# Grouped-query attention on a cache: K loaded in 32 KiB rows, two units in interleaved partitions, with another load order

## The chip, the cores and the metric

The kernel runs on one core of a Trainium2 chip. The metric is the device time of one execution in microseconds (us); less is better. The core has five engines that run side by side, each through its own list of instructions in order: TensorE (PE, matrix products), VectorE (DVE), ScalarE (ACT), GpSimd (POOL) and SyncE (SP), which here issues every transfer between the chip's main memory (HBM) and the on-chip memory (SBUF, 128 partitions). The transfers are carried out by sixteen DMA engines that all work on one queue: each transfer is dealt out over them, and each works through its share of one transfer after the other. TensorE's results land in a small memory of their own, PSUM.

## The reference

Eight sequences (B), four new tokens each (Sq), 32 query heads that share 8 key/value heads, a cache of 2048 keys (Sk), head size 128, bf16:

```python
q = (x @ wq).reshape(B, Sq, Hq, Dh).transpose(0, 2, 1, 3)
k = jnp.repeat(k_cache, rep, axis=1)          # rep = 4
v = jnp.repeat(v_cache, rep, axis=1)
scores = jnp.einsum("bhqd,bhkd->bhqk", q, k) * (Dh ** -0.5)
p = softmax(scores, axis=-1)
o = jnp.einsum("bhqk,bhkd->bhqd", p, v)
out = o.transpose(0, 2, 1, 3).reshape(B, Sq, Hq * Dh) @ wo
```

k_cache and v_cache are 33.5 MB each, wq and wo 4.2 MB each: 75.5 MB are read in all.

## The kernel before

**Units.** The work is cut into 16 units (NU). A unit is one sequence b and four key/value heads (G = 4, one half hq of the eight), so 64 rows of queries (NQ: 4 heads, 4 repeats, 4 tokens) against 2048 keys per head. Its K is 2 MiB, and so is its V. In SBUF, partition (g, s) of a K or V load holds 64 consecutive keys of head g (C = 64 keys of 128 numbers, 16 KiB in one run).

**Stages of a unit.** (1) `turn_keys` (L141): VectorE turns K in blocks of 32 by 32, seen as 4-byte pairs, two tiles of 32 keys per partition. (2) `scores` (L211): per tile eight matmuls of 512 columns against the block-diagonal queries `q_bd`; the two halves of a tile go to PSUM partitions 0 to 63 and 64 to 127. (3) `maxima` (L232) on VectorE: the row maximum, two small copies that swap the halves, and one operation that makes the bias `less`. (4) `exponentials` (L251) on ScalarE, with the row sums. (5) `probs_to_keys` (L262): one turn of the probabilities on VectorE, then eight copies, half on ScalarE and half on GpSimd, into a block-diagonal `probs` buffer (two of them). (6) `values` (L297): 32 matmuls on TensorE in four quarters. (7) `divide` (ScalarE) by the row sums, whose reciprocals `inverses` (VectorE) makes from `sums` (GpSimd); `finish` turns the result back (one or two matmuls and a copy).

**Order.** The order of the instructions on each engine is the order in which the program writes them (the scheduler is switched to manual). The loop at L394 runs over n: it turns and scores unit n, spreads the probabilities of unit n - 1, takes the maxima and exponentials of n, and does the values of unit n - 2 (LAG = 2). Unit 0's two tiles are turned ahead of the loop, L148.

**Loads.** All go through SP's queue in program order, and an instruction of SP that waits holds up those behind it. K has three buffers of one unit (KB), V three (VB). The list `loads` (L115) alternates K and V, K of unit u ahead of V of unit u - 2, and `load_ready` issues each as soon as the program has passed the last use of its buffer; K0, wq, x and one load of K1 with K2 are issued ahead. x lands in one of the three buffers of turned keys. After the last V the output weights wo follow in pieces, in the memory that wq had (L433).

**End.** `project` (L382) multiplies by wo, piece by piece in the order of the loads, once the last unit is finished and turned to rows (`to_tokens`, `to_wo_rows`).

Of the kernel before, what the change touches and what calls it, by code (L numbers as in the profile page):

```python
# [14 lines left out]
def kernel(  # L15
# [23 lines left out]
    NT, CT = 2, C // 2  # L39
# [5 lines left out]
    KB, VB, PB, LAG = 3, 3, 2, 2  # L45
# [11 lines left out]
    vpool = ctx.enter_context(tc.tile_pool(name="vpool", bufs=VB))  # L57
# [11 lines left out]
    x_sb = ktpool.tile([128, CT, 2, S, 2], BF16, tag="kt", name="x_sb")  # L69
# [12 lines left out]
    ks = [None] * NU  # L82
    vs = [None] * NU

    k_sb = kpool.tile([128, KB, C, Dh], BF16, name="k_sb")

    def load_k(u, n=1):
        hq, b = units[u]
        nc.sync.dma_start(
            k_sb[:, u % KB : u % KB + n, :, :].rearrange("p b c d -> p b (c d)"),  # L90
            k_cache[b : b + n, G * hq : G * hq + G].rearrange(
                "b g (s c) d -> (g s) b (c d)", c=C
            ),
        )
        for i in range(n):
            ks[u + i] = k_sb[:, (u + i) % KB, :, :]

    def load_v(u):
        hq, b = units[u]
        vs[u] = vpool.tile([128, C, Dh], BF16, tag="v_sb", name="v_sb")  # L100
        of = v_cache[b, G * hq : G * hq + G].rearrange("g (s c) d -> (g s) c d", c=C)
        nc.sync.dma_start(vs[u][:, :, :], of)
# [8 lines left out]
    x_all = x_sb[:T, :, :, :, :].rearrange("q c h s e -> q (c h s e)")  # L111
    nc.vector.memset(x_all, 0.0)  # L112
    nc.sync.dma_start(x_all[::XR, :], x.flatten_outer_dims().rearrange("(a i) d -> a (i d)", i=XR))
    load_k(1, 2)
    loads = [("v", 0)]  # L115
    for u in range(3, NU + 2):
        if u < NU:
            loads.append(("k", u))
        loads.append(("v", u - 2))
    loads.reverse()  # L120

    def load_ready(nk, nv):
        while loads:
            kind, u = loads[-1]
            if u >= (nk + KB if kind == "k" else nv + VB):
                return
            (load_k if kind == "k" else load_v)(u)
            loads.pop()

    load_ready(0, 0)  # L130
# [10 lines left out]
    def turn_keys(u, t):  # L141
        kts[(u, t)] = ktpool.tile([128, CT, 2, S, 2], BF16, tag="kt", name="kt")
        nc.vector.transpose(  # L143
            kts[(u, t)][:, :, :, :, :].rearrange("k c h s e -> k (c h s e)").bitcast(FP32),
            ks[u][:, t * CT : (t + 1) * CT, :].rearrange("s c d -> s (c d)").bitcast(FP32),
        )

    for t in range(NT):  # L148
        turn_keys(0, t)
# [12 lines left out]
    nc.vector.tensor_copy(out=xT_sb[:, :, :], in_=xtp[:, :, :])  # L162

# [47 lines left out]
    def scores(u, t):  # L211
        hq, b = units[u]
        if t == 0:
            s_pss[u] = psum_s.tile([128, NT, CT // 2, S], FP32, tag="s", name="s_ps")
        for i in range(4):
            k, e = i // 2, i % 2
            for h in range(2):
                nc.tensor.matmul(  # L218
                    s_pss[u][h * NQ : (h + 1) * NQ, t, :, :],
                    lhsT=q_bd[:, hq, k, e, b, :, :].rearrange("k g q -> k (g q)"),  # L220
                    rhs=kts[(u, t)][:, h * CT // 2 : (h + 1) * CT // 2, k, :, e],
                    start=(i == 0),
                    stop=(i == 3),
                )
# [7 lines left out]
    def maxima(u):  # L232
# [5 lines left out]
            in_=s_pss[u][:, :, :, :].rearrange("q t c s -> q (t c s)"),  # L238
# [12 lines left out]
    def exponentials(u):  # L251
# [3 lines left out]
            out=s_sbs[u][:, :, :, :].rearrange("q a s j -> q a j s"),  # L255
            in_=s_pss[u][:, :, :, :].rearrange("q t (a j) s -> q (t a) j s", j=2),
# [5 lines left out]
    def probs_to_keys(u):  # L262
        p_t = small.tile([128, C // 4, 2, HQ, 2], BF16, tag="p_t", name="p_t")
        nc.vector.transpose(  # L264
            p_t[:, :, :, :, :].rearrange("s x g q j -> s (x g q j)").bitcast(FP32),
            s_sbs[u][:, :, :, :].rearrange("q a s j -> q (a s j)").bitcast(FP32),
        )
        by = [nc.scalar.copy, nc.gpsimd.tensor_copy] * G
        if u == NU - 1:
            by = [nc.vector.tensor_copy, nc.gpsimd.tensor_copy, nc.scalar.copy] * 3  # L270
        for h in range(2):
            for g in range(G):
# [3 lines left out]
                    in_=p_t[quad * S : (quad + 1) * S, :, g % 2, :, :].rearrange(  # L276
# [20 lines left out]
    def values(u, quarter):  # L297
        if quarter == 0:
            o_pss[u] = psum_o.tile([128, 2, Dh], FP32, tag="o", name="o_ps")
        t, h = quarter // 2, quarter % 2  # L300
        for a in range(CT // 4):
# [3 lines left out]
                lhsT=probs[u % PB][:, h, t * CT // 4 + a, :, :, :].rearrange(  # L305
# [87 lines left out]
    pieces = [(0, 0, 8), (1, 0, 8), (2, 0, 8), (3, 0, 5), (3, 5, 2), (3, 7, 1)]  # L393
    for n in range(NU + LAG):  # L394
        w = n - LAG
        if 0 < n <= NU:
            total = sums(n - 1)
        if 0 < n < NU:
            turn_keys(n, 0)
            turn_keys(n, 1)  # L400
        if n < NU:
            scores(n, 0)
        if w >= 1 and n < NU:
            finish(w - 1)
        if n < NU:
            scores(n, 1)
        if n == 2:
            q_ps = q_products(1)
        if n == 3:
            spread_q(1, q_nat, [by_gpsimd] * G)  # L410
        if 0 < n <= NU:
            probs_to_keys(n - 1)
            inverses(n - 1, total)
        if n < NU:
            maxima(n)
            exponentials(n)
        if n == 2:
            q_nat = scale_q(q_ps)
        if w == B + 1:
            to_tokens(0)  # L420
        if w == B + 2:
            to_wo_rows(0)
        if w >= 0:
            for quarter in range(4):
                values(w, quarter)
            if n >= NU:
# [52 lines left out]
```

## Time and profile before

| | |
|---|---|
| Time, median of 3 runs | 185.19 us (185.16 to 185.51) |
| The profiled execution | 185.0 us |
| Its span, first to last instruction | 183.1 us |
| DMA | 75.70 MB, mean 413 GB/s over the span |
| VectorE busy | 121.2 us (66%), 72.0 of it in 32 turns of K tiles |
| TensorE matmuls busy | 123.2 us (67%) |
| ScalarE busy | 77.9 us (43%) |
| GpSimd busy | 59.3 us (32%) |
| Mean granted TensorE clock | 0.925 of full speed |

The busy time of an engine is an average over stages with different limits, so what counts for a change is read in the stage that it touches: the chain of waits (the work that ended last, followed back) and the timelines. The DMA line of the page divides the span into 40 slices and gives the busy share of each in tenths, 9 being 90% or more; the line under it gives the rate in each slice. Times in timelines count from the start of the span.

### The profile page before, as it was taken

The page shows a single profiled execution, that of the slowest core. Times are in us where ns is not written, and L with a number is a line of the kernel's source. Part 1 is how long each engine was busy: PE and PEld are TensorE (multiplying, and loading weights), DVE is VectorE, ACT ScalarE, POOL GpSimd, SP SyncE. Part 2 cuts the span into 40 slices and gives each one's busy share as a digit, 9 for nine tenths or more (in the row PEclk, how much of TensorE's full clock was granted, in tenths as well). Part 3 has the DMA queues.
Part 4 walks back from the last instruction along what each step waited for, and adds up shares of the span by engine and source line. Part 5 has one row for each costly group of instructions (what it writes and reads, how often), then busy time and mean ns, then how long its engine had stood idle before and what let it go on. Part 6 is the DMA issues. An engine that isn't in the chain of part 4 may idle for free.

```text
span 183.1 us, 2559 instructions
## 1 busy us (share of the span) xinstructions
PE 123.2 (67%) x962; PEld 80.4 (44%) x962; DVE 121.2 (66%) x157; ACT 77.9 (43%) x136; POOL 59.3 (32%) x127
## 2 busy tenths in 40 slices
PE   0000652709997978869396878397776978399993
PEld 0000320303664736647154455256463656268872
DVE  6380027797989899894967768576948594946120
ACT  2000112264547748548154544529281719075030
POOL 8900020343237525415151514224240506056000
PEclk9999999995899999999969699969997599969999
DMA  6989999999999999999999999999999999999991
GB/s 182 497 386 419 426 433 429 433 433 426 429 429 437 429 431 420 438 419 437 426 433 429 433 426 437 422 437 433 426 433 429 429 433 426 433 426 422 426 392 49
DMA packets 5666, 75.70 MB, mean 413 GB/s; under 512 B 628, under 2 KB 788, under 8 KB 1044
## 3 DMA queue, kind: packets, MB, share of 16 engines
q1 hardware_dynamic: 5656, 75.57, 97.1%
q8 instruction: 7, 0.11, 0.2%
q14 instruction: 3, 0.02, 0.0%
HBM read 75.53 MB, written 0.03 MB: 413 GB/s over the span
## 4 chain that ended last, share of the span: by engine, by line
DMA 58%; DVE 23%; PE 13%; issue 1%; SPq 1%; POOL 1%; ACT 0%
DMA k_sb<-in_k_cache_dram 38%; DVE kt L143 17%; DMA wo_sb<-in_wo_dram 12%; DMA x_sb<-in_x_dram 8%; PE s_ps L218 6%; PE o_ps L303 4%; DVE top L236 3%; PE psq L169 2%; DVE x_sb L112 1%; SPq L107 1%; POOL q_bd L195 1%; DVE q_t L189 1%; PE out_ps L385 1%; DVE swapped L228 1%; PE xtp L155 1%
## 5 line engine op out<-in xcount | busy, mean ns | idle before, releaser
L143 DVE STREAM_TRANSPOSE kt<-k_sb 128x2048 f32<-128x2048 f32 x32 | 72.0, 2288 | 17.8 <-DMA k_sb<-in_k_cache_dram 17.8
L218 PE MATMUL s_ps<-kt,q_bd 128*64 128x512 bf16 x256 | 44.3, 477 | 37.5 <-DVE kt L143 34.6
L303 PE MATMUL o_ps<-v_sb,probs 128*128 128x256 bf16 x512 | 62.4, 284 | 0.3 <-ACT oT L341 0.3
L274 ACT COPY probs<-p_t 32x512 bf16<-32x512 bf16 x62 | 38.1, 615 | 52.8 <-DVE r_sb L292 51.7
L303 PEld LDWEIGHTS <-probs 128*128 128x128 bf16 x512 | 50.9, 102 | 15.1 <-issue 6.7
L274 POOL COPY probs<-p_t 32x512 bf16<-32x512 bf16 x63 | 38.6, 613 | 56.6 <-DVE r_sb L292 54.3
L218 PEld LDWEIGHTS <-q_bd 128*64 128x64 bf16 x256 | 16.9, 125 | 55.1 <-issue 24.7
L236 DVE TENSOR_REDUCE top<-s_ps 128x1 f32<-128x1024 f32 x16 | 19.6, 1223 | 16.0 <-PE s_ps L218 16.0
L254 ACT ACTIVATE s_sb<-s_ps,less 128x1024 bf16<-128x1024 f32 x16 | 22.4, 1399 | 10.6 <-DVE less L242 10.4
L228 POOL COPY l_swapped<-l_sb 64x1 f32<-64x1 f32 x32 | 5.8, 181 | 32.0 <-ACT s_sb L254 31.3
L155 PE MATMUL xtp<-ident,x_sb 32*128 32x4 bf16 x32 | 1.2, 169 | 18.7 <-DMA x_sb<-in_x_dram 18.7
L323 ACT ACTIVATE o_sc<-o_ps,r_sb 64x128 f32<-64x128 f32 x28 | 10.1, 362 | 7.5 <-PE o_ps L303 6.8
L264 DVE STREAM_TRANSPOSE p_t<-s_sb 128x512 f32<-128x512 f32 x16 | 11.0, 689 | 1.6 <-ACT s_sb L254 1.6
L195 POOL COPY q_bd<-q_t 32x512 bf16<-32x512 bf16 x6 | 3.8, 626 | 18.7 <-DVE q_t L189 18.6
L180 ACT ACTIVATE q_nat<-psq 128x512 bf16<-128x512 f32 x2 | 1.2, 590 | 20.2 <-PE psq L169 20.2
L155 PEld LDWEIGHTS <-x_sb 32*128 32x128 bf16 x32 | 1.1, 112 | 18.7 <-issue 18.7
L340 PEld LDWEIGHTS o_t<-both,o_sc 128*128 128x128 f32 x30 | 4.9, 205 | 6.1 <-issue 4.8
L136 POOL MEMSET probs<- 128x4096 bf16 x2 | 7.0, 3513 | 0.0
L340 PE MATMUL o_t<-both,o_sc 128*128 128x64 f32 x30 | 6.8, 312 | 0.0
L341 DVE CAST oT<-o_t 128x64 bf16<-128x64 f32 x14 | 2.7, 193 | 4.7 <-PE o_t L340 4.7
L228 DVE COPY swapped<-top 64x1 f32<-64x1 f32 x32 | 4.7, 148 | 0.8
L162 DVE CAST xT_sb<-xtp 128x128 bf16<-128x128 f32 x1 | 0.3, 291 | 7.0 <-PE xtp L155 7.0
(37 smaller groups left out, 46.0 us busy)
## 6 DMA issues: line engine op xcount, KB each, us to landing
v_sb<-in_v_cache_dram SPq DMA_DIRECT2D x16, 2048.0 KB, 23.3
k_sb<-in_k_cache_dram SPq DMA_DIRECT2D x14, 2048.0 KB, 23.5
wq_sb<-in_wq_dram SPq DMA_DIRECT2D x1, 4096.0 KB, 17.2
k_sb<-in_k_cache_dram SPq DMA_DIRECT2D x1, 4096.0 KB, 24.3
wo_sb<-in_wo_dram SPq DMA_DIRECT2D x3, 1024.0 KB, 18.9
wo_sb<-in_wo_dram SPq DMA_DIRECT2D x1, 640.0 KB, 21.9
wo_sb<-in_wo_dram SPq DMA_DIRECT2D x1, 256.0 KB, 22.0
wo_sb<-in_wo_dram SPq DMA_DIRECT2D x1, 128.0 KB, 19.6
```

The costliest lines, as they stand in the source:

```text
L136: nc.gpsimd.memset(pr[:, :, :, :, :, :], 0.0)
L143: nc.vector.transpose(kts[(u, t)][:, :, :, :, :].rearrange("k c h s e -> k (c h s e)").bitcast(FP32), ks[u][:, t * CT : (t + 1) * CT, :].r ...
L195: engines[g](out=q_bd[rows, hq, :, :, :, g, :].rearrange("w k e b (h s) -> w (k e b) h s", h=rep), in_=q_t[rows, :, :, :, :].rearrange("w ...
L218: nc.tensor.matmul(s_pss[u][h * NQ : (h + 1) * NQ, t, :, :], lhsT=q_bd[:, hq, k, e, b, :, :].rearrange("k g q -> k (g q)"), rhs=kts[(u, t) ...
L228: engine.tensor_copy(out=out[h * NQ : (h + 1) * NQ, :], in_=in_[(1 - h) * NQ : (2 - h) * NQ, :])
L236: nc.vector.reduce_max(out=top[:, :], in_=s_pss[u][:, :, :, :].rearrange("q t c s -> q (t c s)"), axis=AX,)
L254: nc.scalar.activation(out=s_sbs[u][:, :, :, :].rearrange("q a s j -> q a j s"), in_=s_pss[u][:, :, :, :].rearrange("q t (a j) s -> q (t a ...
L264: nc.vector.transpose(p_t[:, :, :, :, :].rearrange("s x g q j -> s (x g q j)").bitcast(FP32), s_sbs[u][:, :, :, :].rearrange("q a s j -> q ...
L274: by[h * G + g](out=probs[u % PB][g * S : (g + 1) * S, h, :, :, g, :], in_=p_t[quad * S : (quad + 1) * S, :, g % 2, :, :].rearrange("s x q ...
L303: nc.tensor.matmul(o_pss[u][:, :, :].rearrange("n j d -> n (j d)"), lhsT=probs[u % PB][:, h, t * CT // 4 + a, :, :, :].rearrange("s j g q ...
L323: nc.scalar.mul(out=to, in_=of, mul=by)
L340: nc.tensor.matmul(o_t[:, :], lhsT=o_scs[u][:, :], rhs=both[:, :], start=True, stop=True)
```

## The change

K is loaded in rows of 128 keys (32 KiB in one run), so a unit's K fills 64 partitions and not 128. Two units form a pair: the even one takes the even partitions, the odd one the odd partitions of one buffer; there are two such buffers (KB = 2, each as large as two of the old). One turn of a tile serves both units of the pair, and a pair has four tiles (NT = 4). A score matmul reads every second column group of a turned tile (`j::2`), and the two units' matmuls alternate; a unit's scores lie in PSUM as (i, c, s), i being the half of the tiles, and the exponential reads them in the order (c, s, i). V has two buffers; V12 and V13 go to the K buffer that the last pair but one leaves. x lands in V's first buffer. The loop runs over pairs: the turns of a pair come first, the reciprocals of all units that wait follow, the turn of the probabilities is separated from the copies (`turn_probs`, `copy_probs`), and the order of loads and values is written out (`loads_after`, `values_of`). A V load stands one block later in the queue than in the loop before. The values of the last four units follow the loop. The last quarter of wo is loaded in pieces of 6 and 2 rows and not 5, 2 and 1.

```diff
@@ -39 +39,3 @@
-    NT, CT = 2, C // 2
+    NT, CT = 4, C // 2
+    CP = 2 * C
+    SH = S // 2
@@ -45 +47,2 @@
-    KB, VB, PB, LAG = 3, 3, 2, 2
+    KB, VB, PB, LAG = 2, 2, 2, 2
+    NPAIR = NU // 2
@@ -57 +60 @@
-    vpool = ctx.enter_context(tc.tile_pool(name="vpool", bufs=VB))
+    vpool = ctx.enter_context(tc.tile_pool(name="vpool", bufs=1))
@@ -69 +71,0 @@
-    x_sb = ktpool.tile([128, CT, 2, S, 2], BF16, tag="kt", name="x_sb")
@@ -82,2 +84,6 @@
-    ks = [None] * NU
-    vs = [None] * NU
+    k_sb = [kpool.tile([128, CP, Dh], BF16, name=f"k_sb{i}") for i in range(KB)]
+    v_sb = [vpool.tile([128, C, Dh], BF16, name=f"v_sb{i}") for i in range(VB)]
+    spare = k_sb[(NPAIR - 2) % KB]
+    vs = [v_sb[u % VB][:, :, :] for u in range(NU)]
+    for i, u in enumerate((NU - 4, NU - 3)):
+        vs[u] = spare[:, i * C : (i + 1) * C, :]
@@ -85,3 +91 @@
-    k_sb = kpool.tile([128, KB, C, Dh], BF16, name="k_sb")
-
-    def load_k(u, n=1):
+    def load_k(u):
@@ -90,4 +94,2 @@
-            k_sb[:, u % KB : u % KB + n, :, :].rearrange("p b c d -> p b (c d)"),
-            k_cache[b : b + n, G * hq : G * hq + G].rearrange(
-                "b g (s c) d -> (g s) b (c d)", c=C
-            ),
+            k_sb[u // 2 % KB][u % 2 :: 2, :, :],
+            k_cache[b, G * hq : G * hq + G].rearrange("g (s c) d -> (g s) c d", c=CP),
@@ -95,2 +97,4 @@
-        for i in range(n):
-            ks[u + i] = k_sb[:, (u + i) % KB, :, :]
+
+    def load_pair(p):
+        load_k(2 * p)
+        load_k(2 * p + 1)
@@ -100,3 +104,3 @@
-        vs[u] = vpool.tile([128, C, Dh], BF16, tag="v_sb", name="v_sb")
-        of = v_cache[b, G * hq : G * hq + G].rearrange("g (s c) d -> (g s) c d", c=C)
-        nc.sync.dma_start(vs[u][:, :, :], of)
+        nc.sync.dma_start(
+            vs[u], v_cache[b, G * hq : G * hq + G].rearrange("g (s c) d -> (g s) c d", c=C)
+        )
@@ -111 +115 @@
-    x_all = x_sb[:T, :, :, :, :].rearrange("q c h s e -> q (c h s e)")
+    x_all = v_sb[0][:T, :, :].rearrange("q c d -> q (c d)")[:, : XR * D]
@@ -114,17 +118,2 @@
-    load_k(1, 2)
-    loads = [("v", 0)]
-    for u in range(3, NU + 2):
-        if u < NU:
-            loads.append(("k", u))
-        loads.append(("v", u - 2))
-    loads.reverse()
-
-    def load_ready(nk, nv):
-        while loads:
-            kind, u = loads[-1]
-            if u >= (nk + KB if kind == "k" else nv + VB):
-                return
-            (load_k if kind == "k" else load_v)(u)
-            loads.pop()
-
-    load_ready(0, 0)
+    load_k(1)
+    load_pair(1)
@@ -141,2 +130,2 @@
-    def turn_keys(u, t):
-        kts[(u, t)] = ktpool.tile([128, CT, 2, S, 2], BF16, tag="kt", name="kt")
+    def turn_keys(p, t):
+        kts[(p, t)] = ktpool.tile([128, CT, 2, S, 2], BF16, tag="kt", name="kt")
@@ -144,2 +133,2 @@
-            kts[(u, t)][:, :, :, :, :].rearrange("k c h s e -> k (c h s e)").bitcast(FP32),
-            ks[u][:, t * CT : (t + 1) * CT, :].rearrange("s c d -> s (c d)").bitcast(FP32),
+            kts[(p, t)][:, :, :, :, :].rearrange("k c h s e -> k (c h s e)").bitcast(FP32),
+            k_sb[p % KB][:, t * CT : (t + 1) * CT, :].rearrange("s c d -> s (c d)").bitcast(FP32),
@@ -148,3 +136,0 @@
-    for t in range(NT):
-        turn_keys(0, t)
-
@@ -162,0 +149 @@
+    load_v(0)
@@ -211,2 +198,2 @@
-    def scores(u, t):
-        hq, b = units[u]
+    def scores(p, t):
+        pair = (2 * p, 2 * p + 1)
@@ -214 +201,2 @@
-            s_pss[u] = psum_s.tile([128, NT, CT // 2, S], FP32, tag="s", name="s_ps")
+            for u in pair:
+                s_pss[u] = psum_s.tile([128, 2, CT, SH], FP32, tag="s", name="s_ps")
@@ -217 +205,3 @@
-            for h in range(2):
+            for j, u in enumerate(pair):
+                hq, b = units[u]
+                h = (t + j) % 2
@@ -219 +209 @@
-                    s_pss[u][h * NQ : (h + 1) * NQ, t, :, :],
+                    s_pss[u][h * NQ : (h + 1) * NQ, t // 2, :, :],
@@ -221 +211 @@
-                    rhs=kts[(u, t)][:, h * CT // 2 : (h + 1) * CT // 2, k, :, e],
+                    rhs=kts[(p, t)][:, :, k, j::2, e],
@@ -238 +228 @@
-            in_=s_pss[u][:, :, :, :].rearrange("q t c s -> q (t c s)"),
+            in_=s_pss[u][:, :, :, :].rearrange("q i c s -> q (i c s)"),
@@ -255,2 +245,2 @@
-            out=s_sbs[u][:, :, :, :].rearrange("q a s j -> q a j s"),
-            in_=s_pss[u][:, :, :, :].rearrange("q t (a j) s -> q (t a) j s", j=2),
+            out=s_sbs[u][:, :, :, :].rearrange("q a w j -> q a j w"),
+            in_=s_pss[u][:, :, :, :].rearrange("q i c s -> q c s i"),
@@ -262,2 +252,4 @@
-    def probs_to_keys(u):
-        p_t = small.tile([128, C // 4, 2, HQ, 2], BF16, tag="p_t", name="p_t")
+    p_ts = {}
+
+    def turn_probs(u):
+        p_ts[u] = small.tile([128, C // 4, 2, HQ, 2], BF16, tag="p_t", name="p_t")
@@ -265 +257 @@
-            p_t[:, :, :, :, :].rearrange("s x g q j -> s (x g q j)").bitcast(FP32),
+            p_ts[u][:, :, :, :, :].rearrange("s x g q j -> s (x g q j)").bitcast(FP32),
@@ -267,0 +260,2 @@
+
+    def copy_probs(u):
@@ -276 +270 @@
-                    in_=p_t[quad * S : (quad + 1) * S, :, g % 2, :, :].rearrange(
+                    in_=p_ts[u][quad * S : (quad + 1) * S, :, g % 2, :, :].rearrange(
@@ -300,2 +294,2 @@
-        t, h = quarter // 2, quarter % 2
-        for a in range(CT // 4):
+        h, a0 = (quarter // 2 + u) % 2, quarter % 2 * (C // 8)
+        for a in range(C // 8):
@@ -305 +299 @@
-                lhsT=probs[u % PB][:, h, t * CT // 4 + a, :, :, :].rearrange(
+                lhsT=probs[u % PB][:, h, a0 + a, :, :, :].rearrange(
@@ -393,17 +387,36 @@
-    pieces = [(0, 0, 8), (1, 0, 8), (2, 0, 8), (3, 0, 5), (3, 5, 2), (3, 7, 1)]
-    for n in range(NU + LAG):
-        w = n - LAG
-        if 0 < n <= NU:
-            total = sums(n - 1)
-        if 0 < n < NU:
-            turn_keys(n, 0)
-            turn_keys(n, 1)
-        if n < NU:
-            scores(n, 0)
-        if w >= 1 and n < NU:
-            finish(w - 1)
-        if n < NU:
-            scores(n, 1)
-        if n == 2:
-            q_ps = q_products(1)
-        if n == 3:
+    pieces = [(0, 0, 8), (1, 0, 8), (2, 0, 8), (3, 0, 6), (3, 6, 2)]
+
+    waiting = []
+
+    def spread(u):
+        waiting.append((u, sums(u)))
+        copy_probs(u)
+
+    def all_inverses():
+        while waiting:
+            inverses(*waiting.pop(0))
+
+    def softmax_top(u):
+        maxima(u)
+        exponentials(u)
+
+    values_of = [(), (0,)] + [(2 * p - 3, 2 * p - 2) for p in range(2, NPAIR - 2)]
+    values_of += [(NU - 7,), (NU - 6, NU - 5)]
+    loads_after = [("p2",), ("v1", "v2", "p3")]
+    loads_after += [(f"v{2 * p - 1}", f"v{2 * p}", f"p{p + 2}") for p in range(2, NPAIR - 3)]
+    loads_after += [("v9", "p7", "v10"), ("v11", "v12", "v13"), ("v14", "v15")]
+    turned = 0
+    done = None
+    for p in range(NPAIR):
+        last = p == NPAIR - 1
+        vals = values_of[p]
+        turn_keys(p, 0)
+        turn_keys(p, 1)
+        all_inverses()
+        scores(p, 0)
+        if done is not None:
+            finish(done)
+        scores(p, 1)
+        if p == 0:
+            q_nat = scale_q(q_products(1))
+        if p == 1:
@@ -411,9 +424 @@
-        if 0 < n <= NU:
-            probs_to_keys(n - 1)
-            inverses(n - 1, total)
-        if n < NU:
-            maxima(n)
-            exponentials(n)
-        if n == 2:
-            q_nat = scale_q(q_ps)
-        if w == B + 1:
+        if p == NPAIR - 2:
@@ -421 +426,9 @@
-        if w == B + 2:
+        for quarter in range(2) if vals else ():
+            values(vals[0], quarter)
+        turn_keys(p, 2)
+        scores(p, 2)
+        turn_keys(p, 3)
+        scores(p, 3)
+        for quarter in (2, 3) if vals else ():
+            values(vals[0], quarter)
+        if p == NPAIR - 2:
@@ -423 +436,19 @@
-        if w >= 0:
+        while turned < (2 * p if p else 0):
+            turn_probs(turned)
+            turned += 1
+        softmax_top(2 * p)
+        if vals:
+            divide(vals[0])
+        softmax_top(2 * p + 1)
+        if p == 0:
+            for u in range(2):
+                turn_probs(u)
+                spread(u)
+            turned = 2
+        elif p == 1:
+            turn_probs(2)
+            spread(2)
+            turned = 3
+        else:
+            spread(vals[0] + 2)
+        if len(vals) > 1:
@@ -425,9 +456,24 @@
-                values(w, quarter)
-            if n >= NU:
-                finish(w - 1)
-            (divide_all if w == NU - 1 else divide)(w)
-        load_ready(min(n + 1, NU), max(w + 1, 0))
-        if n == NU - 1:
-            assert not loads, loads
-            for piece in pieces:
-                load_wo(*piece)
+                values(vals[1], quarter)
+                if quarter == 1:
+                    finish(vals[0])
+            divide(vals[1])
+            while turned < vals[1] + 3:
+                turn_probs(turned)
+                turned += 1
+            spread(vals[1] + 2)
+        done = vals[-1] if vals else None
+        for load in loads_after[p]:
+            (load_pair if load[0] == "p" else load_v)(int(load[1:]))
+    for piece in pieces:
+        load_wo(*piece)
+    for w in range(NU - 4, NU):
+        all_inverses()
+        for quarter in range(4):
+            values(w, quarter)
+        finish(w - 1)
+        (divide_all if w == NU - 1 else divide)(w)
+        if w + 2 < NU:
+            while turned < w + 3:
+                turn_probs(turned)
+                turned += 1
+            spread(w + 2)
```

## The prediction

> **What bounds the kernel now.** I read the slices of the span first, then the DMA queues, the chain of waits, and the timelines of VectorE and TensorE up to 75 us.
>
> ```profile
> DMA  6989999999999999999999999999999999999991
> GB/s 182 497 386 419 426 433 429 433 433 426 429 429 437 429 431 420 438 419 437 426 433 429 433 426 437 422 437 433 426 433 429 429 433 426 433 426 422 426 392 49
> q1 hardware_dynamic: 5656, 75.57, 97.1%
> q8 instruction: 7, 0.11, 0.2%
> ```
>
> The sixteen DMA engines are busy from the second slice to the last but one, at about 430 GB/s. A load of 2048 KB ("a unit" below; wq and wo are two each) is 4.85 us. No engine's work ends last for long; what counts is whether the queue ever runs dry, and a dry microsecond never comes back.
>
> ```profile
> 67.23 20.18 DMA k_sb<-in_k_cache_dram
> ...
> 91.97 24.68 DMA k_sb<-in_k_cache_dram
> ...
> 157.12 21.87 DMA wo_sb<-in_wo_dram
> 178.99 0.04 issue
> 179.04 1.25 PE out_ps L385 x16
> ```
>
> From the chain of waits (start, length, what): from 67 us on, VectorE waits for K; each load lands over 20 us after its issue, so four to five units are always queued. That depth is the cover which the change spends. At the end wo's fourth piece lands at 178.99 and sixteen matmuls follow.
>
> ```profile
> 22.87 0.71 DVE L189 STREAM_TRANSPOSE q_t<-q_nat 128x512 bf16<-128x512 bf16 x1 [2.63 <-ACT q_nat L180]
> 23.62 0.28 DVE L195 COPY q_bd<-q_t 32x512 bf16<-32x512 bf16 x1
> 28.76 1.23 DVE L236 TENSOR_REDUCE top<-s_ps 128x1 f32<-128x1024 f32 x1 [4.86 <-PE s_ps L218]
> 30.02 0.31 DVE L228 COPY swapped<-top 64x1 f32<-64x1 f32 x2
> 30.37 0.21 DVE L242 TENSOR_SCALAR less<-swapped,top 128x1 f32<-128x1 f32 x1
> 30.50 4.49 DVE L143 STREAM_TRANSPOSE kt<-k_sb 128x2048 f32<-128x2048 f32 x2
> 34.91 0.67 DVE L264 STREAM_TRANSPOSE p_t<-s_sb 128x512 f32<-128x512 f32 x1
> ```
>
> VectorE's timeline (start, length): a turn of a K tile is 2.23 us, a softmax top 1.75 (1.23 + 0.31 + 0.21), a turn of the probabilities 0.63. The first scores cannot start before q_bd is there, about 24 us.
>
> ```profile
> 43.28 1.92 PE L218 MATMUL s_ps<-kt,q_bd 128*64 128x512 bf16 x8 [0.27 <-DVE kt L143]
> 50.66 1.10 PE L218 MATMUL s_ps<-kt,q_bd 128*64 128x512 bf16 x8
> 60.87 3.67 PE L303 MATMUL o_ps<-v_sb,probs 128*128 128x256 bf16 x32
> ```
>
> On TensorE the eight score matmuls of a tile take 1.92 or 1.10 us, by the clock, and a unit's values 3.67 at the high one.
>
> **The change, part by part.**
>
> *Longer rows.* In the trace's packet records a 16 KiB packet starts 607 ns after the last of its engine, a 32 KiB one (wq's rows) 1209. K goes from 2048 packets to 1024, so 64 pairs per engine save 5 ns each: 0.3 us. If the rows are cut to 16 KiB after all, this is nothing.
>
> *Half the partitions.* A K load now writes 64 partitions, every second one. No row shows such a load; the nearest are the 128-partition loads at full rate (cost nothing) and, as the other bound, half rate (+4.85 us for each of 16). I take full rate: the stride reaches over all 128 partitions and the queue cuts the same bytes into whole rows. The bound is a rival below.
>
> *The first units.* Before, unit 0 is turned at 8.44 to 12.9, while VectorE waits for x. Now both tiles of unit 0 and both of unit 1 stand behind q_bd and need K1, which lands at about 23.2 (wq at 18.4 plus 4.85). So the hidden 4.5 us come onto the path, and the first softmax comes after four turns and not after two. Step by step: q_bd done on VectorE 23.9; four turns, 32.8; the last tile's scores 1.1 to 1.9 (TensorE also carries the second q product, 1.9), 34.4; first top, 36.2; exponential 1.57 (1.39 and its read of 0.18); second top, 37.9; its exponential, 39.6; turn of the probabilities, 40.2; four turns of pair 1 and the second q_t (0.7), 49.9. The scores of those tiles and the first half of unit 0's values fit between; after the last turn follow 1.1 of scores and 1.84 of values, partly behind what TensorE still owes: unit 0's values end at 53.0.
>
> *Two V buffers, and the queue's order.* The order is now K0, wq, x, K1, K2, K3, V0, K4, K5, V1, V2, K6, K7, V3 and so on. V0 waits for x's use (19.9 us) under 15 us of queued K: free. K4 and K5 wait for pair 0's turns (32.9), V0 covers them to 37: free. V2 takes V0's buffer, so SP waits at V2 until 53.0, and K6, K7 stand behind it although their buffer is free at 50. Before, with three V buffers, V2 went out at 35.39 and the next K at 43.26. Ahead of V2 lie ten units, as many as before up to V2 itself, which landed at 53.45 (K8, seven units on, at 87.42, less 7 × 4.85). The landing records spread: the first engine had done its part at 51.65, one was 1.8 later. From issue to first packet takes 0.95 to 1.05 (K0: issued 0.73, first packet 1.78; the output, 0.87). So V2's data starts at 54.0 and most engines idle 2.4 us. V3 waits for unit 1's values: by the same steps 68.0, data 69.0, against 68.6 for K7's end: 0.4 more (0.1 to 1.0, by where the clock steps). V4 and later are issued in time: block p needs 12 us from K's landing to the release of the next V, the queue then holds 19.4 (four units), so 6 us and more are spare. That margin hides the later edits too (probabilities turned ahead, reciprocals a pair later: the same numbers of instructions, moved by at most a block); without it each would cost its own 0.1 to 1.3 us.
>
> The trace's clock decides about 1 us of this: if TensorE is at the low clock at 50 us, 1.8 us later. [...]
>
> *Other reads.* The score matmuls read every second element pair of a tile (step 8 bytes for 4), the exponential alternates between two halves of its scores. No row shows either. Bounds: as now (0.24 us a matmul pair at the low clock, 1.39) or twice that; as a gain, nothing, since counts and sizes stay. I take them as now, nearest in shape. Twice the exponential would put V2 back by 1.8, twice the scores by about 8.
>
> *The wo end.* The fourth piece grows from five to six rows: 128 KB more, 0.3 us later (179.3), and still sixteen matmuls (1.25) follow: +0.3; bounds 0 (the last piece landed at 179.9 in either) and 0.3.
>
> *Late engines.* The spread at K0's landing (7.87 to 8.42) is wiped out when all engines start V2 together, and only the instruction fetches' lag (1.2 on one engine each) builds up anew: −0.3.
>
> Sum: +2.4 + 0.4 − 0.3 + 0.3 − 0.3 = +2.5. The profiled execution took 185.0 us (183.1 of span), 0.2 under the median of 185.19. Forecast 187.5, to which I add 0.1 as the unknown reads can only lose: 187.6; its own range 186.3 to 189.5.
>
> **Rivals.**
>
> *The queue does not run dry (0.18; 184.9).* It decides on whether V2 is issued before 50.7 (51.65 less 0.95). Then only rows (−0.3) and end (0 to +0.3) are left: 184.7 to 185.2. For it: 2.3 us out of a chain of 30, built of rows at two clocks. Against: VectorE's own work alone, eight turns, two tops, two turns of probabilities and q_t from 23.9, is 23.3 us, 47.2; two waits that cannot be hidden (scores 1.1, exponential 1.3) and the last scores and values (2.9) make 52.5.
>
> *The strided reads cost (0.14; 191).* If the exponential takes 2.5 instead of 1.57, V2 loses 1.1 more, V3 1.4, V4 0.7: about 191; scores at twice the time bring 195 and more. For: both patterns are new. Against: ACT is 43% busy and TensorE's matmuls read with a step already.
>
> *Half-width K loads (0.08; 263).* If two engines at a time write to the same part of the memory, each K unit takes 9.7: 16 × 4.85 = 78 us more, and no gap at V2. For: never run here. Against: the partitions are spread over the whole memory. [...]
>
> The forecast has 0.60. About 0.2% is what a measurement of this kernel can tell from no change (184.8 to 185.6). Faster 0.12, same 0.06, both out of the first rival; slower 0.82. The range 185.0 to 193 leaves out the half-width case (0.08) and the faster end (0.1).
>
> **What would show it.** A slice near 54 us with clearly less than 430 GB/s; SP waiting for values at V2 with an issue at 52 to 54 and the first V2 packet a microsecond later; 32 KiB packets at 1213 ns; K landings 9.7 apart after that, with VectorE waiting on K as before; the last matmuls 0.3 us later after the fourth piece. I am wrong if V2 goes out before 50.7, if the exponential or the scores are longer than 1.6 and 1.92, or if K's packets take longer than wq's.

## The result, and the profile after

The changed kernel takes 197.66 us (median of 4 runs, 196.88 to 198.78) against 185.18 (185.09 to 185.51) of the kernel before on the same chip: a ratio of 1.0675, 95% interval 1.0621 to 1.0729. The forecast had been 187.6. The profiled execution took 197.52, with a span of 195.5; spans are compared with the 183.1 of before.

The page of the changed kernel: the DMA engines' busy share and rate in 40 slices of 4.9 us, then the queue, then the engines' shares of the chain that ended last.

```profile
DMA  6999999999559978999999999999999999999960
GB/s 215 429 429 436 429 429 409 453 429 409 235 151 486 436 262 355 359 473 426 391 429 463 436 406 432 473 429 389 469 426 392 429 429 436 349 355 414 429 260 7
q1 hardware_dynamic: 4504, 75.57, 92.3%
PE 44%; DMA 28%; DVE 19%; issue 3%; ACT 3%; SPq 1%; ACTq 0%
```

The queue, full from end to end before, has a hole in slices 11 and 12 (49 to 59 us), a smaller one in slices 15 to 17, and a dip of the rate (349 and 355 GB/s) in slices 35 and 36. K's longer rows show in the count of packets, 4504 for 5656. The chain is now led by TensorE with 44%, where before DMA led with 58% (K's landings alone 38%). The windows give the size of the holes (stretch and its length; then for PE, weight loads, DVE, ACT and POOL the busy time and the number of instructions; granted clock, DMA share, GB/s):

```profile
48.00:60.00 12.00, 7.41 (x47) 3.60 (x47) 9.31 (x13) 4.78 (x9) 3.74 (x9) 0.90 0.63 239
66.00:80.00 14.00, 12.12 (x80) 6.55 (x80) 10.27 (x17) 7.84 (x15) 5.80 (x14) 1.00 0.87 328
```

37% of 12 us are 4.4 us without data, and 13% of 14 are 1.8; before, both stretches had a share of 1.00. The timeline of SP (start, length, what) says why:

```profile
55.04 0.33 SPq L104 DMA_DIRECT2D v_sb<-in_v_cache_dram  x1
55.47 1.12 SPq L93 DMA_DIRECT2D k_sb<-in_k_cache_dram  x2
71.84 4.76 SPq L104 DMA_DIRECT2D v_sb<-in_v_cache_dram  x2
```

V2 goes out at 55.04 and V3 at 71.84, each after its wait for the values that free its buffer. The forecast had this wait, with 53.0 and 68.0. The reason for the difference stands in the groups of instructions (busy time, mean ns of one | idle time before them), the first line from the kernel before, the others from the changed one:

```profile
L218 PE MATMUL s_ps<-kt,q_bd 128*64 128x512 bf16 x256 | 44.3, 477 | 37.5 <-DVE kt L143 34.6
L208 PE MATMUL s_ps<-kt,q_bd 128*64 128x512 bf16 x256 | 62.3, 627 | 33.3 <-DVE kt L132 33.3
L132 DVE STREAM_TRANSPOSE kt<-k_sb 128x2048 f32<-128x2048 f32 x32 | 71.7, 2282 | 6.7 <-DMA k_sb<-in_k_cache_dram 6.7
L244 ACT ACTIVATE s_sb<-s_ps,less 128x1024 bf16<-128x1024 f32 x16 | 22.4, 1400 | 65.9 <-PE o_ps L297 60.3
```

The score matmuls take 627 ns each and not 477; as they overlap, TensorE is busy with them for 62.3 us and not 44.3. What is new in their reads is `j::2`: it takes every second column inside each group of 32 columns (a step of 8 bytes where there were 4), not every second group. Turns (2282 ns; 2288 before) and exponentials (1400; 1399) are what they were, so the exponential's alternating read costs nothing. TensorE's timeline ahead of V2:

```profile
49.33 3.83 PE L208 MATMUL s_ps<-kt,q_bd 128*64 128x512 bf16 x16
53.09 1.92 PE L297 MATMUL o_ps<-v_sb,probs 128*128 128x256 bf16 x16
```

Sixteen values in 1.92 us are values at the high clock (granted 1.00 from 49.3 to 55.0 us; 32 took 3.67 before). At that clock eight scores took 1.10 before, and here sixteen take 3.83, which is 1.92 for eight. At a granted clock of 0.50 eight took 1.92 before (from 43.28 us) and take 2.00 to 2.04 here (from 59.60 and 62.19 us), so the difference shows almost only at the full clock.

The end of the span, on TensorE:

```profile
179.32 3.66 PE L297 MATMUL o_ps<-v_sb,probs 128*128 128x256 bf16 x32
182.98 3.66 PE L297 MATMUL o_ps<-v_sb,probs 128*128 128x256 bf16 x32
...
190.24 2.36 PE L379 MATMUL out_ps<-wo_sb,oP 128*32 128x256 bf16 x40
```

No wait for wo is left ahead of the last matmuls: four units' values and then `project` run through to 192.6, where before the last sixteen matmuls waited for wo's landing and ended at 180.3.

### The profile page after: what moved, and what is told of

It is laid out like the page before. It is cut to its first block, busy times and chain, and to the rows that moved or that the text cites. A ratio compares the mean times of both kernels' runs of the same rounds, so it can differ in the third digit from the quotient of the medians.

```text
span 195.5 us, 2563 instructions
## 1 busy us (share of the span) xinstructions
PE 136.3 (70%) x962; PEld 76.5 (39%) x962; DVE 121.3 (62%) x157; ACT 76.7 (39%) x136; POOL 59.1 (30%) x127
## 3 DMA queue, kind: packets, MB, share of 16 engines
q1 hardware_dynamic: 4504, 75.57, 92.3%
## 4 chain that ended last, share of the span: by engine, by line
PE 44%; DMA 28%; DVE 19%; issue 3%; ACT 3%; SPq 1%; ACTq 0%
PE s_ps L208 22%; DMA k_sb<-in_k_cache_dram 20%; PE o_ps L297 15%; DVE kt L132 9%; DMA v_sb<-in_x_dram 8%; DVE top L226 6%; PE o_t L334 2%; PE out_ps L379 2%; ACT s_sb L244 2%; PE psq L156 1%; DVE swapped L218 1%; ACT o_sc L317 1%; DVE v_sb L116 1%; DVE less L232 1%; PE xtp L141 1%
## 5 line engine op out<-in xcount | busy, mean ns | idle before, releaser
L208 PE MATMUL s_ps<-kt,q_bd 128*64 128x512 bf16 x256 | 62.3, 627 | 33.3 <-DVE kt L132 33.3
L132 DVE STREAM_TRANSPOSE kt<-k_sb 128x2048 f32<-128x2048 f32 x32 | 71.7, 2282 | 6.7 <-DMA k_sb<-in_k_cache_dram 6.7
L297 PEld LDWEIGHTS <-probs 128*128 128x128 bf16 x512 | 48.9, 99 | 18.7 <-issue 12.1
L297 PE MATMUL o_ps<-v_sb,probs 128*128 128x256 bf16 x448 | 52.8, 274 | 0.0
L208 PEld LDWEIGHTS <-q_bd 128*64 128x64 bf16 x256 | 15.7, 128 | 64.9 <-issue 32.7
L141 PE MATMUL xtp<-ident,v_sb 32*128 32x4 bf16 x32 | 1.2, 169 | 18.9 <-DMA v_sb<-in_x_dram 18.9
L141 PEld LDWEIGHTS <-v_sb 32*128 32x128 bf16 x32 | 1.1, 111 | 18.8 <-issue 18.8
L297 PE MATMUL o_ps<-k_sb,probs 128*128 128x256 bf16 x64 | 7.3, 273 | 1.2 <-PE o_t L334 0.8
L281 POOL TENSOR_TENSOR l_total<-l_sb,l_swapped 128x1 f32<-128x1 f32 x16 | 3.0, 190 | 13.6 <-DVE r_sb L286 12.6
## 6 DMA issues: line engine op xcount, KB each, us to landing
v_sb<-in_v_cache_dram SPq DMA_DIRECT2D x14, 2048.0 KB, 10.2
```

The costliest lines, as they stand in the source:

```text
L132: nc.vector.transpose(kts[(p, t)][:, :, :, :, :].rearrange("k c h s e -> k (c h s e)").bitcast(FP32), k_sb[p % KB][:, t * CT : (t + 1) * C ...
L141: nc.tensor.matmul(xtp[:, r, i::XR], lhsT=row[:, r, :], rhs=ident[:T, :T:XR], start=True, stop=True,)
L208: nc.tensor.matmul(s_pss[u][h * NQ : (h + 1) * NQ, t // 2, :, :], lhsT=q_bd[:, hq, k, e, b, :, :].rearrange("k g q -> k (g q)"), rhs=kts[( ...
L297: nc.tensor.matmul(o_pss[u][:, :, :].rearrange("n j d -> n (j d)"), lhsT=probs[u % PB][:, h, a0 + a, :, :, :].rearrange("s j g q -> s (j g q)"
```

## The experiments

Kernels of one batch share their runs of the kernel before, whose medians lay between 185.02 and 185.18.

**1. The two units' columns sorted by the turn.** The turn writes the even and the odd unit's columns apart, so that a score matmul reads runs of 16 with a step of 4 bytes, as before.

```diff
-        kts[(p, t)] = ktpool.tile([128, CT, 2, S, 2], BF16, tag="kt", name="kt")
+        kts[(p, t)] = ktpool.tile([128, CT, 2, 2, SH, 2], BF16, tag="kt", name="kt")
...
+            .rearrange("k c h j w e -> k (c h j w e)")
+            .bitcast(FP32)
+            .rearrange("k (x j w) -> k x w j", j=2, w=SH),
...
-                    rhs=kts[(p, t)][:, :, k, j::2, e],
+                    rhs=kts[(p, t)][:, :, k, j, :, e],
```

> The changed kernel, with the turn writing the two units' columns apart, so that the score matmuls read with a step of 4 bytes again (runs of 16). Theory (the step of 8 bytes holds the score matmuls at 1.92 us per eight whatever the clock): 1.10 to 1.15 us at the high clock, turns unchanged at 2.23, V2 issued at 53 and not at 55, the tail no longer set by TensorE, time 187 to 188.5, near the forecast. Rival (the alternation of two units' matmuls and not the step): 1.92 stays, 197 to 198. Second rival (the turn pays for its scattered write): turns of 3 us or more, time above 192.

Measured: 216.11 us (215.42 to 217.69), ratio 1.1666 (1.1645 to 1.1686). The groups of instructions of this kernel:

```profile
L132 DVE STREAM_TRANSPOSE kt<-k_sb 128x2048 f32<-128x2048 f32 x32 | 113.2, 3612 | 2.3 <-DMA k_sb<-in_k_cache_dram 2.2
L214 PE MATMUL s_ps<-kt,q_bd 128*64 128x512 bf16 x256 | 48.0, 508 | 59.8 <-DVE kt L132 55.8
```

TensorE's timeline in a stretch of full granted clock:

```profile
60.24 1.06 PE L214 MATMUL s_ps<-kt,q_bd 128*64 128x512 bf16 x8 [2.40 <-DVE kt L132]
```

The scores are short again, although they read in runs of 16, as short as those of the `j::2` reads; so the length of the runs is not what made them long. But the second rival came true: the turn, which now scatters its writes, takes 3612 ns for 2282, 41 us more on VectorE in all. The cost moved from TensorE to VectorE, where it is larger, so the run does not answer what the step costs the kernel.

**2. The reads near again, the turn left alone.** Each unit's matmul reads half of a tile's column groups in full, with the step of 4 bytes.

```diff
-                    rhs=kts[(p, t)][:, :, k, j::2, e],
+                    rhs=kts[(p, t)][:, j * CT // 2 : (j + 1) * CT // 2, k, :, e],
```

> The changed kernel, each score matmul reading 16 of the 32 column groups of a tile in full (step 4 bytes, runs of 32) instead of every second column of all: a unit then scores half of the keys of both units, so the values are others. Theory of the step: 1.10 us per eight, 187 to 188.5. Rival (alternation): 1.92 and 197 to 198. If this is fast and the kernel with the sorted turn is not, the length of the runs counts.

Measured: 190.99 us (one run), a span of 188.9. V2's issue on SP, and the scores just ahead of it on TensorE:

```profile
52.64 0.33 SPq L104 DMA_DIRECT2D v_sb<-in_v_cache_dram  x1
```

```profile
49.63 1.13 PE L208 MATMUL s_ps<-kt,q_bd 128*64 128x512 bf16 x8 [0.16 <-DVE kt L132]
```

With the scores as short as the forecast took them, V2 goes out at 52.64, where the forecast's chain had 53.0. The two units' matmuls still alternate here, so it is not the alternation that made them long. The step is worth 6.7 us (a single run, against four runs of the changed kernel that spread over 1.9). What remains above the kernel before, 5.9, is more than the forecast's 2.5.

**3. The step alone, in the kernel before.**

```diff
-                    rhs=kts[(u, t)][:, h * CT // 2 : (h + 1) * CT // 2, k, :, e],
+                    rhs=kts[(u, t)][:, :, k, h::2, e],
```

> The kernel before, with the step alone: each half of a tile's score matmuls reads every second column (step 8 bytes) instead of half of the column groups, so keys are summed in another order than V's. Theory of the step: 1.92 us per eight at either clock, and the time hardly moves, 185 to 186.2, since the queue of loads stays four to five units deep. Rival (alternation of units): 1.10 at the high clock, 185.2.

Measured: 185.01 us (184.94 to 185.10), ratio 0.9994 (0.9985 to 1.0003). The scores did get longer, as TensorE's timeline shows in a stretch of full granted clock:

```profile
58.71 1.90 PE L218 MATMUL s_ps<-kt,q_bd 128*64 128x512 bf16 x8 [0.53 <-DVE kt L143]
```

The same longer instruction costs nothing in the kernel before and 6.7 us in the changed one. In the kernel before, the longer scores are covered: VectorE waits less for K (10.2 us in all, for 17.8), and the queue stays full. In the changed one the queue waits for the chain in which the scores stand.

**4. K in two halves of the partitions.** The even unit goes to partitions 0 to 63, the odd one to 64 to 127. This was built on the kernel of experiment 1, not on the changed one, so it is read against 216.11.

```diff
-            k_sb[u // 2 % KB][u % 2 :: 2, :, :],
+            k_sb[u // 2 % KB][u % 2 * 64 : u % 2 * 64 + 64, :, :],
```

> The changed kernel, with the even unit of a pair in partitions 0 to 63 and the odd one in 64 to 127 (keys then meet other queries; the values are others). If 64 neighbouring partitions load at half rate: a K load of 9.7 us where the interleaved one takes 4.85, 32 KiB packets of about 2400 ns, time above 250. Rival (any 64 partitions load at full rate): packets of 1213 ns and 197 to 198.

Measured: 290.47 us (one run), 74.4 more than experiment 1; sixteen loads at half rate would be 16 × 4.85 = 78. The rates on its page:

```profile
GB/s 182 250 436 227 218 209 200 291 243 218 191 393 302 205 211 301 362 202 218 185 393 266 214 186 282 364 216 218 198 275 214 211 200 384 434 225 345 411 408 10
```

The stretches of K run at 200 to 220 GB/s, those of V at up to 436, and a 32 KiB packet of K takes 2562 ns (median of the packet records) where the changed kernel's takes 1213, the time of a wq row before. So 64 neighbouring partitions were filled at half rate and 64 that alternate at full rate: the forecast took the right one. That two engines at a time write to the same part of the memory, as the rival has it, no run shows.

**5. wq in two column halves.** The half that unit 0 needs goes ahead of x, the other behind K1, so the first chain starts earlier; the step stays.

```diff
-    nc.sync.dma_start(wq_sb[:, :, :], wq.rearrange("(p r) n -> p r n", r=R))
+    half_q = HqDh // 2
+    def load_wq(i):
+        cols = slice(i * half_q, (i + 1) * half_q)
+        nc.sync.dma_start(
+            wq_sb[:, :, cols], wq.rearrange("(p r) n -> p r n", r=R)[:, :, cols]
+        )
+    load_wq(0)
...
     load_k(1)
+    load_wq(1)
```

> The changed kernel, with wq loaded in two halves of columns (the half for the first eight units ahead of x, the other behind K1), so that x, q_bd and all of VectorE's first chain come one unit, 4.85 us, earlier at the same place of the queue. Theory (the queue runs dry at V2 and V3 since VectorE's first chain, begun by q_bd, is too long): V2 issued at 50.2 and not at 55.1, the dry spells at 51 to 58 and 70 to 74 gone or under 1 us together, the stretched packets after them gone too, the end set by TensorE's last block, 187 to 189. Rival (what is dry is given by K's arrival and the order of the queue, not by the chain): still dry for 4 us and more, 195 to 198.

Measured: 194.84 us (193.97 to 195.07), ratio 1.0514 (1.0487 to 1.0540). V2 goes out at 50.6 and the first hole is gone, but not the time: the second hole stays. Its windows, columns as above:

```profile
48.00:60.00 12.00, 7.41 (x40) 3.26 (x37) 10.61 (x14) 5.83 (x10) 3.54 (x10) 0.74 1.02 423
66.00:80.00 14.00, 12.13 (x85) 7.14 (x84) 12.72 (x17) 9.03 (x16) 5.97 (x14) 1.00 0.91 348
```

V3 is late by itself, though V2 went out 4.4 us earlier than in the changed kernel. The time lies just under the rival's 195 and at least 5.8 us above what the theory expected: taking away the first hole is not enough while the scores are long.

**6. Both: near reads and wq in halves.** The edits of 2 and 5 together.

> As e5, and the scores read whole column groups (step 4 bytes), which mixes the two units' keys as in e2. Theory: no dry spell, and TensorE's last block ends with the loads: 185.0 to 186. Rival (the tail is set by the order of the last blocks and not by the scores' length): TensorE ends 1 us and more after the last load, 186 to 187.5.

Measured: 186.47 us (185.98 to 186.66), ratio 1.0071 (1.0054 to 1.0088). V2 goes out at 47.83, and the DMA line of its page shows no hole:

```profile
DMA  6899999999999989999999999999999999999980
```

So step and first chain together hold 11.2 of the 12.5 us: 6.7 by experiment 2, and from there 4.5 more here. The shares depend on the order: with the halves of wq first (experiment 5) it is 2.8 and then 8.4. The time is in the rival's range, and TensorE does end last: its last matmul ends at 181.3, the last packet of wo at 180.0.

**7. K6 and K7 ahead of V2,** with near reads.

```diff
-    loads_after = [("p2",), ("v1", "v2", "p3")]
+    loads_after = [("p2",), ("v1", "p3", "v2")]
```

> As e2, with V2 issued behind K6 and K7. Theory of VectorE's chain: the place in the queue does not matter, since V3 then finds the queue dry instead of V2: a dry spell of 2.5 to 3 us near 66 us, time 190 to 191.5. Rival (V2 holds K6 and K7 back, and that is the loss): no dry spell over 0.5 us, 187.5 to 188.5.

Measured: 190.32 us (one run), against the 190.99 of experiment 2. The DMA line shows the hole moved, not filled:

```profile
DMA  7999999999999959999999999999999999999970
```

V2 goes out at 53.03, and the hole now lies between 66 and 70 us (DMA share 0.53 there), as the theory had it. Whichever load waits, the queue waits for VectorE's chain behind q_bd; the order only says when it shows. The 0.67 between two single runs says nothing about the better order.

**8. The wo pieces 6 and 2 alone, in the kernel before.**

```diff
-    pieces = [(0, 0, 8), (1, 0, 8), (2, 0, 8), (3, 0, 5), (3, 5, 2), (3, 7, 1)]
+    pieces = [(0, 0, 8), (1, 0, 8), (2, 0, 8), (3, 0, 6), (3, 6, 2)]
```

> The kernel before, with the last quarter of wo in pieces of 6 and 2 rows alone. Theory of the prediction: sixteen matmuls follow a piece that lands 0.3 us later, so 0.3 us more: 185.4. Rival (the last landing, at 179.9 in either, sets the end): 185.1.

Measured: 185.27 us (185.16 to 185.45), ratio 1.0010 (1.0001 to 1.0019): +0.16, between the two expectations. The last sixteen matmuls start at 179.40 for 179.04.

**9 and 10. Other steps, in the kernel before.** The same number of columns, read with a step of 16 bytes, and in runs of 32 neighbours.

```diff
-                    rhs=kts[(u, t)][:, h * CT // 2 : (h + 1) * CT // 2, k, :, e],
+                    rhs=kts[(u, t)][:, :, :, 2 * k + h :: 4, e],
```

```diff
+                    rhs=kts[(u, t)][:, h * CT // 2 : (h + 1) * CT // 2, k, e * 16 : e * 16 + 16, :],
```

> The kernel before, with score matmuls that read every fourth column (step 16 bytes, 512 columns as before), both k parts of a tile in one matmul, so the sums are of other numbers. If the reading rate halves with each doubling of the step: 3.8 us per eight matmuls, VectorE held up and the time above 190. Rival (a step over 4 bytes costs once, whatever its length): 1.92 us per eight, 185.

> The kernel before, with score matmuls that read runs of 32 neighbouring numbers (step 2 bytes, 512 columns as before), again other sums. If the step of 4 bytes is already without cost: 1.10 us per eight at the high clock as before, 185. Rival (the 4-byte step costs something too): under 1.0.

Measured (one run each): 233.04 us with 16 bytes, 185.09 with neighbours. TensorE's timelines at full granted clock, first with 16 bytes, then with neighbours:

```profile
60.14 3.77 PE L218 MATMUL s_ps<-kt,q_bd 128*64 128x512 bf16 x8
```

```profile
51.84 1.05 PE L218 MATMUL s_ps<-kt,q_bd 128*64 128x512 bf16 x8
```

For eight matmuls of 512 columns at the full clock: step 2 bytes 1.05, 4 bytes 1.05 to 1.13, 8 bytes 1.90, 16 bytes 3.77. From 4 bytes on, the time nearly doubled with each of these doublings of the step. Experiment 9 also shows that the cover of the kernel before is finite: VectorE's wait for K is down to 3.0 us from 17.8, and the kernel takes 48 us more.

**11. The tail, first try.** Experiment 6 with wo in 5, 2 and 1 rows, and `to_wo_rows(0)` behind the second exponential of its block.

```diff
-    pieces = [(0, 0, 8), (1, 0, 8), (2, 0, 8), (3, 0, 6), (3, 6, 2)]
+    pieces = [(0, 0, 8), (1, 0, 8), (2, 0, 8), (3, 0, 5), (3, 5, 2), (3, 7, 1)]
...
-        if p == NPAIR - 2:
-            to_wo_rows(0)
         while turned < (2 * p if p else 0):
...
         softmax_top(2 * p + 1)
+        if p == NPAIR - 2:
+            to_wo_rows(0)
```

> As e6, with wo's end in pieces of 5, 2 and 1 rows again and with the step that puts the first half's results into rows of wo moved behind the second exponential of its block, so that ScalarE's exponentials do not stand behind copies that wait for TensorE. Theory (the rest of the loss after e6 is the last blocks' chain, begun too late): TensorE starts the last block's scores 1 us earlier and ends with the loads: 185.0 to 185.6. Rival (the chain is bound elsewhere in the last two blocks): 186 to 186.5 as in e6.

Measured: 186.91 us (185.78 to 187.60), ratio 1.0080 (1.0056 to 1.0103): no gain is shown. In the profiled execution (187.60, the longest of six) TensorE fell to the low clock in the last blocks (granted 0.50 in the stretch of this line):

```profile
148.66 3.59 PE L306 MATMUL o_ps<-v_sb,probs 128*128 128x256 bf16 x16
```

These sixteen values took 3.59 us where 1.92 is usual. The runs spread over 1.8 us, which hides what the edit did. The theory missed.

**12. The tail, second try: less work there.** Experiment 6, with every second matmul of the last four units' values left out.

```diff
-        for a in range(C // 8):
+        step = 2 if u >= NU - 4 else 1
+        for a in range(0, C // 8, step):
...
-                stop=(c == C - 2),
+                stop=(c == C - 2 * step),
```

> The kernel with step-4 reads and wq in two halves (186.47 us, no dry spell, yet 1.36 over the kernel before). Here the values of the last four units use every second of their matmuls, so half of these units' keys is left out: 4 x 16 matmuls of 0.115 us, 7.3 us of TensorE's work behind the last scores, are gone; loads, their order and all else stay. Theory: the end is TensorE's, because four units' values (4 x 3.66 us) follow the last scores without a gap and its last matmuls end at 181.3, some 1 us behind the last landing. Then the end falls back to the last piece of wo and its sixteen matmuls: 185.1 plus the 0.16 of the pieces of 6 and 2, with 0 to 0.3 for packets that are stretched, so 185.2 to 185.6, and the chain of waits ends with wo's landing. Rival: the loads themselves end later than before by the 1 us, and TensorE only fills the time: 186.2 to 186.7, with a wait for wo ahead of the last matmuls.

Measured: 185.86 us (185.73 to 186.24), ratio 1.0045 (1.0032 to 1.0057), which lies between the two expectations. TensorE's last matmuls in experiment 6, and then here:

```profile
178.92 2.36 PE L388 MATMUL out_ps<-wo_sb,oP 128*32 128x256 bf16 x40
```

```profile
179.65 1.05 PE L389 MATMUL out_ps<-wo_sb,oP 128*32 128x256 bf16 x16 [0.79 <-DMA wo_sb<-in_wo_dram]
```

With less work the end is wo's landing again, as before the change, though at 179.65 and not at 179.04. So TensorE's tail holds 0.5 us (1.36 less 0.84 over the kernel before), and the last big piece of wo comes 0.6 later. Of that 0.6, the six rows of the piece account for 0.36 (179.40 in experiment 8). The rest can be the experiment's own. In halves wq is 1024 packets of 4 KiB, which start 155 ns apart on an engine, 9.9 us over sixteen engines, for 128 rows of 32 KiB at 1209, 9.7; by this estimate the halves cost 0.25.

## Why the prediction was wrong, step by step

**The step that failed: "Other reads ... I take them as now, nearest in shape".** The exponential bore it out. The scores did not: eight at the full clock went from 1.10 to 1.92 us, a term that the sum had at nothing (0.1 for both reads), and it was worth 6.7 of the 12.5 us. The other bound named beside it, twice as long, was nearly the truth, though "twice the scores by about 8" overstated how far V2 would go back: it was 2.4 us later than in experiment 2. The rival that had scores at twice the time bring 195 and more was right as well. It got 0.14 together with the exponential, and the range ended at 193, short of its own figure. The weak link was the argument against it, that the matmuls read with a step already: a step of 4 bytes costs next to nothing (1.05 to 1.13 us for the 1.05 of neighbours) and a step of 8 does (1.90). The low clock (granted 0.50) hid this, since there eight scores took 1.92 us already. The sign of being wrong, scores longer than 1.92, was set at that low-clock time, so the long scores at the full clock, 1.92 as well, do not trip it.

**The first units: right, and the size of each step nearly so.** The four turns ended at 33.0 (forecast 32.8). The last scores ahead of the first top put that 1.0 late (35.4 for 34.4). Of this, 0.8 is left at the end of the next four turns (50.7 for 49.9), and the long scores behind them add the other 1.3 up to V2's issue. With near reads V2 is within 0.4 of the forecast. That the clock decides about 1 us here was the author's estimate; over the chain's last stretch it was the full one (granted 1.00 from 49.3 to 55.0 us). The 0.1 to 1.0 at V3, by where the clock steps, was an estimate too; V3 went out at 71.84 for 68.0, behind a stretch at the low clock (granted 0.50 from 57.7 to 64.4 us). Experiment 7 confirms that this chain, not the order of the loads, sets the hole.

**What an empty queue costs: mis-sized.** The forecast took an empty queue as lost only for as long as it is empty, and even counted −0.3 for engines that start together. The packet records give, as a mean over the sixteen engines, two figures: the idle time between 5 us and the first packet of wo's fourth piece, and the time by which packets of 16 and 32 KiB run over their usual 611 and 1213 ns.

| | idle | packets too long |
|---|---|---|
| kernel before | none | 1.3 |
| changed kernel | 6.6 | 4.6 |
| experiment 2 | 2.5 | 2.9 |
| experiment 5 | 2.5 | 5.9 |
| experiment 6 | none | 1.3 |

The long packets of the kernel before are nearly all at the start of the span. In the others, most come right behind a hole, and some behind a load that came only just in time (experiment 5, 108 to 112 us: 0.8 with hardly any idle). Experiment 2, with scores as short as the forecast took them, still ends 3.4 us above the forecast of 187.6. Its idle time, 2.5, is about what the forecast had (2.4 + 0.4), and 1.6 of long packets come on top; the rest of the 3.4 is open. That long packets follow a hole is a correlation of the records, not an experiment by itself.

**The margin of 6 us behind V3: wrong with long scores.** From V5 to V13 no load came late, but from 160 to 176 us the DMA share is 0.96 (1.00 in experiment 2), and the queue ran dry at V3 in experiment 5 with the first hole gone. The block's 12 us had been reckoned with short scores.

**The end: the wrong engine.** The sixteen matmuls that "still" follow wo's last big piece were taken from the kernel before. With four units' values behind the last scores, TensorE ends last: the last matmul moved by 12.3 us, the landing of wo's big piece by 10.3. Experiment 12 shows the tail to be TensorE's at 0.5 us once the holes are gone.

**Two slips that moved nothing.** Eight scores in 1.92 us are 0.24 a matmul, not a pair. And the times of the first rival, 184.7 to 185.2, lie mostly within what counts as no change (184.8 to 185.6), yet "faster" got twice the chance of "same" out of it.

**Right:** longer rows (16 KiB at 611, 32 KiB at 1213 ns, half the packets for K; the −0.3 itself is too small to be seen here); half the partitions at full rate, and so no half-width loads; the wo end's bounds (+0.16, within 0 to 0.3, though 0.3 was counted).

**The account.** 197.66 to 190.99 by near reads, to 186.47 by an earlier start of the first chain, to 185.86 by less work behind the last scores; by the last step a part of the work is left out, so it measures the tail and is no kernel to use. Of the 0.84 left over the 185.02 beside it, 0.16 is the wo pieces, an estimated 0.25 the halves of wq, and some 0.4 is open. No version beat the kernel before: the longer rows, 0.3 us by the packet records, are worth too little to pay for the lost depth.

## What to carry to other kernels

A new access pattern of an operand is to be priced anew, and at the high clock (a step of 8 bytes for 4 took eight scores from 1.10 us to 1.92, while the exponential's alternating read left it at 1400 ns): ask for the step in bytes between the columns that a matmul reads. Whether a longer instruction costs time is decided by what waits for its chain: the same scores were free ahead of a full queue and cost 6.7 us where the queue's next load stood behind them. When buffers are made larger and fewer, work out the first two blocks instruction by instruction, and then the last two, since here the holes in a full queue came with longer packets (4.6 us beside 6.6 of idle time) and with a late tail.

## What the runs showed of the hardware

- Eight score matmuls of 512 columns took 1.05 us at the full clock with a step of 2 bytes between the columns of their moving operand (`rhs`), 1.05 to 1.13 with 4 bytes, 1.90 with 8 and 3.77 with 16: from 4 to 8 and from 8 to 16 the time nearly doubled.
- The step of 8 bytes showed almost only at the full clock: with it eight scores took 1.93 to 2.04 us at a granted clock of 0.50 and 1.90 to 1.92 at the full one, without it 1.92 and 1.05 to 1.13.
- K loads into 64 neighbouring partitions took 2562 ns for a packet of 32 KiB, into every second partition 1213.
- The 32 by 32 turn of a K tile (128x2048 4-byte pairs) that scattered its writes took 3612 ns, the one that did not 2282.
- The exponential (128x1024) that reads alternately from two halves of its scores took 1400 ns, with the order of reads before the change 1399.
